# Softmax sums applied to attention's output instead of its weights, with a new order, in attention fused with a gated MLP

## The chip, the cores and the metric

One core of one Trainium2 chip runs the whole program. The metric is device time in microseconds of one execution; lower is better. In texts and rows, PE is TensorE's matmuls, PEld its weight loads, DVE is VectorE, ACT is ScalarE, POOL is GpSimd and SP is the queue that issues all DMAs.

## What is computed

Causal attention over 4 batches, 12 heads, 448 positions and 64 columns a head, then a gated MLP over the 768 joined columns. The inputs q, k and v are float32; w_in and w_out reach the kernel as 64-bit floats.

```
scores = where(mask, -1e9, q k^T / 8);  attn = exp(scores - max)
attn   = attn / (sum(attn) + 1e-9);     x = attn v      (heads joined: 448 x 768)
h = gelu_tanh(x w_in);  u, v = halves of h (512 columns each)
v = (v - mean) / sqrt(var + 1e-6) * g_ln
out = x + (u * (w_sg v + b_sg)) w_out
```

## The kernel before

**Pairs.** Attention runs for two heads at a time (`pair`, 24 pairs, 6 a batch; z is 0 or 1 for the head). The queries of a head lie in four row chunks (`CH`, line 24): 64 rows with 64 keys, then 128 rows each with 192, 320 and 448 keys, so that the part above the diagonal is mostly left out. A pair loads q and k (L438) and v (L533), and TensorE makes the scores into four PSUM banks (L446). VectorE adds the mask in place and takes the maximum (L459), ScalarE takes exp into an SBUF tile P and the sum of each row (L466). Per head, VectorE copies one sum to other partitions (L475), adds 1e-9 (L479), takes the reciprocal of four numbers a partition (L481), and normalises P: two pieces on VectorE, two on GpSimd (L484). Then TensorE transposes P in nine pieces per head (L501, tiles tx and ty): seven of 128 rows, two of 64 rows. ScalarE and VectorE evict them (L508, L510; the bits of `EV` choose), and TensorE multiplies with v into a bank o (L538). ScalarE copies o to xt (L544); xt is written to DRAM (L549), rounded by ScalarE (L551), and GpSimd subtracts the rounded from the exact values (L552, L554), as x is kept as a sum of two parts for the MLP. There are three P tiles.

**Weights.** Each piece of w_in (12) and w_out (8) is loaded as 64-bit words and turned into two float32 parts (`split_w64`): ScalarE scales the high word (L382), VectorE shifts the low word (L384), joins the two (L386) and puts the sign back (L389), ScalarE rounds (L392) and GpSimd subtracts (L393).

**MLP.** For each batch (`mlp`), four token chunks of the v half (66 matmuls), four groups of the u half (72), four groups with w_sg (44) and six groups with w_out (72), all at L571, in pieces of three matmuls, each group in one PSUM bank. The gelu, the mean and variance and the gating run on the other engines (L579 to L584, L621 to L638, L672 to L679); L702 adds x and the result goes out (L706, L710).

**Order.** Nothing runs in the order in which it is written. Each operation is added to a list (`Order.add`) with its engine, an estimated length, what it reads and writes, and a due time. `plan` places them with these estimates: on each engine, of those that are ready, the one that is due first. It also models PSUM banks (`BANKS`, eight in all), the DMA queue and TensorE's pace. The due times come from `STEP` (the distance of pairs by batch), `MLP` and `LEN` (start and length of each batch's MLP) and `DUE` (offsets by kind). The order that results is fixed when the program is built; every engine and the DMA queue then works through its own list in order.

```
STEP = [6.5, 15.0, 15.0, 15.0]
MLP = [-4.9, 2.6, 52.0, 4.0]
BANKS = dict(s=4, tx=1, ty=2, o=1, m=6)
```

Of the kernel before, what the change touches and what calls it, by code (L numbers as in the profile page):

```python
# [9 lines left out]
F32 = mybir.dt.float32  # L10
# [14 lines left out]
    3: (128, 448, 0, 0, 640, 0, 320),  # L25
    0: (64, 64, 0, 448, 1024, 1, 0),
    2: (128, 320, 1, 192, 256, 2, 192),
    1: (128, 192, 1, 0, 0, 3, 64),
}
PW = 1152  # L30

STEP = [6.5, 15.0, 15.0, 15.0]
MLP = [-4.9, 2.6, 52.0, 4.0]
LEN = [80.0, 88.0, 88.0, 53.0]

EV = 9
# [3 lines left out]
NP, XP = 3, 7  # L40
# [3 lines left out]
BANKS = dict(s=4, tx=1, ty=2, o=1, m=6)  # L44

DUE = dict(load=-9, S=-2, mx=-1, ex=2, inv=-2, norm=3, T=4, ev=-2, V=-2, PV=5,
           xo=0, xs=7.5, post=-2, wv=-8.4, wu=40, wo=80, mu=-8.7, ms=11, mo=48)
# [18 lines left out]
class Order:  # L66
# [17 lines left out]
    def add(self, eng, dur, fn, r=(), w=(), at=0.0, done=0.0, rows=1.0, size=0.0, early=0.0, shape=None):  # L84
# [8 lines left out]
        for k in w:  # L93
# [5 lines left out]
            if wr is not None:  # L99
# [5 lines left out]
                             shape=shape,  # L105
# [4 lines left out]
    def plan(self):  # L110
# [72 lines left out]

        def matmul(t, o):
# [10 lines left out]
        while len(order) < len(ops):  # L195
# [23 lines left out]
            if e == "pe":  # L219
                end = matmul(s + (SHIFT if o["shape"] != shape else 0.0), o)  # L220
                shape = o["shape"]
            else:
                end = s + o["d"]
# [36 lines left out]
def attention_gated_mlp(ctx: ExitStack, tc: tile.TileContext, qk, vP, w_in, g_ln, w_sgT, b_sg, w_out, out):  # L260
# [25 lines left out]
    def bank(tag):  # L286
        return Buf(ps, [128, 512], F32, tag, "b")
# [3 lines left out]
    ident = const.tile([128, 128], F32, name="ident")  # L291
    mask = const.tile([128, S], BF16, name="mask")
    gcol = const.tile([128, FC], F32, name="gcol")
# [7 lines left out]
    sm = [const.tile([128, 4], F32, name=f"sm{i}") for i in range(NP)]  # L301
    rs = [const.tile([128, 4], F32, name=f"rs{i}") for i in range(NP)]
# [14 lines left out]
    def dve(n, fn, r, w, at, rate=1.0417, done=0.0):  # L317
        od.add("dve", 0.068 + n * rate / 1000, fn, r, w, at, done)

    def pool_tt(n, fn, r, w, at):  # L320
        od.add("pool", 0.15 + n * 0.0021, fn, r, w, at)

    def pool_ts(n, fn, r, w, at):
        od.add("pool", 0.245 + n * 0.00083, fn, r, w, at)
# [15 lines left out]
    od.add("pool", 1.0, consts, w=["ident", "mask"], at=-9)  # L340

    def consts2():
        for i in range(NP):
            for c in (192, 576, 1088):
                nc.vector.memset(P[i][:, c:c + 64], 0.0)
            nc.vector.memset(sm[i], 1.0)
# [27 lines left out]
    def split_w64(src, dst, key, n, at, pool_, tag, words):  # L374
# [7 lines left out]
        act(n, lambda: nc.scalar.activation(out=f(hi()), in_=f(hi()), func=AF.Copy, scale=2.0 ** -112),  # L382
            [t], [kh], at, True)
        dve(n, lambda: nc.vector.tensor_scalar(out=lo(), in0=lo(), scalar1=29, scalar2=None,  # L384
                                               op0=ALU.logical_shift_right), [t], [kl], at, 0.53)
        dve(n, lambda: nc.vector.scalar_tensor_tensor(out=lo(), in0=hi(), scalar=3, in1=lo(),  # L386
                                                      op0=ALU.logical_shift_left, op1=ALU.bitwise_or),
            [t, kh], [kl], at)
        dve(n, lambda: nc.vector.scalar_tensor_tensor(out=lo(), in0=hi(), scalar=-(2 ** 31), in1=lo(),  # L389
                                                      op0=ALU.bitwise_and, op1=ALU.bitwise_or),  # L390
            [t, kh], [kl], at)
        act(n, lambda: nc.scalar.activation(out=dst(0), in_=f(lo()), func=AF.Copy), [t, kl], [(key, 0)], at, True)  # L392
# [12 lines left out]
    def weights_b():  # L405
# [10 lines left out]
        dve(600, halve, ["gb"], ["gb"], 40)  # L416
# [14 lines left out]
    def pair(p):  # L431
# [9 lines left out]
        def score(cs):  # L441
            for c in cs:
                m, n, bk, col, _, _, q0 = CH[c]
# [9 lines left out]
        for c in (3, 0, 2, 1):  # L453
            m, n, bk, col, off, k, _ = CH[c]
            for z in range(2):
                def mxs(c=c, m=m, n=n, bk=bk, col=col, z=z):
                    o = s[z][bk].t[0:m, col:col + n]
                    mk = mask[0:m, S - n:S] if m == 128 else mask[0:m, S - 128:S - 64]
# [3 lines left out]
        for c in (3, 0, 2, 1):  # L462
            m, n, bk, col, off, k, _ = CH[c]
            for z in range(2):
                i = ib[z]
                act(n, lambda c=c, m=m, n=n, bk=bk, col=col, off=off, k=k, i=i, z=z: nc.scalar.activation(  # L466
# [293 lines left out]
```

## Time and profile before

| | us |
|---|---|
| median of 3 runs (416.07 to 418.93) | 416.31 |
| the profiled execution | 416.54 |
| its span, from first to last instruction | 414.8 |
| busy: TensorE matmul | 388.4 |
| busy: VectorE | 292.1 |
| busy: ScalarE | 224.4 |
| busy: GpSimd | 185.0 |

The mean granted clock of TensorE is 0.967 of full speed over the span. Busy time is time in which an engine executes instructions; a busy TensorE may be one at half clock. Between the profiled execution's time and its span lie 1.7 us at its ends.

### The profile page before, as it was taken

The numbers are of one execution on the slowest core, as the hardware profiler recorded it, in microseconds if no ns is written. First come the engines' busy times: TensorE is split into PE (matmuls) and PEld (weight loads), VectorE is DVE, ScalarE is ACT, GpSimd is POOL, SyncE is SP. The second block draws the span as 40 slices with busy tenths as digits, with TensorE's granted clock in tenths as the row PEclk, the third lists the DMA queues.
The fourth block names the chain that finished last, engine by engine and source line by source line (L and its number), as shares of the span: only waits on it lengthen the run. The fifth ranks groups of instructions, "written<-read, shape, count | busy, mean of one in ns | idle before, by whom it ended". The sixth has DMA issues, their size and how long they took to land.

```text
span 414.8 us, 6860 instructions
## 1 busy us (share of the span) xinstructions
PE 388.4 (94%) x2226; PEld 296.8 (72%) x2226; DVE 292.1 (70%) x926; ACT 224.4 (54%) x625; POOL 185.0 (45%) x236
## 2 busy tenths in 40 slices
PE   7488889897999999999999999999999999999996
PEld 3345555585766767888877866786778789888995
DVE  3999999999998878626768778746858622263622
ACT  2986687764857577513566667635636731133310
POOL 1565656657625955314132675322331655031440
PEclk9598987989899999999999999999999999999999
DMA  7954655710212233530232324455100111400034
GB/s 264 360 161 169 199 173 203 248 56 2 74 56 93 92 94 109 174 128 1 67 112 95 93 55 153 158 155 172 38 27 0 30 63 44 135 2 2 0 129 139
DMA packets 21239, 44.86 MB, mean 108 GB/s; under 512 B 2514, under 2 KB 12498, under 8 KB 21202
## 3 DMA queue, kind: packets, MB, share of 16 engines
q1 hardware_dynamic: 21202, 44.41, 32.8%
q8 instruction: 18, 0.29, 0.3%
q14 instruction: 19, 0.16, 0.1%
HBM read 33.39 MB, written 11.01 MB: 107 GB/s over the span
## 4 chain that ended last, share of the span: by engine, by line
PE 57%; DVE 19%; ACT 11%; POOL 5%; DMA 4%; issue 3%; DVEq 0%; POOLq 0%; ACTq 0%; SPq 0%
PE m L571 38%; ACT P L466 7%; PE s L446 6%; PE o L538 6%; DVE s L459 4%; PE tx L501 3%; DVE P L484 3%; PE ty L501 3%; DMA tmp<-in_w_sgT_dram 2%; ACT ph L510 2%; POOL P L484 1%; DVE vn L386 1%; DMA res<-xd 1%; DVE gT L389 1%; POOL x L552 1%
## 5 line engine op out<-in xcount | busy, mean ns | idle before, releaser
L466 ACT ACTIVATE P<-s,ngm 128x448 f32<-128x448 f32 (+2 forms) x192 | 88.6, 469 | 33.1 <-DVE ngm L459 20.6
L484 POOL TENSOR_SCALAR P<-P,rs 128x384 f32<-128x384 f32 x96 | 57.7, 615 | 99.7 <-DVE rs L481 67.1
L459 DVE CUSTOM_DVE_ANT_0 s<-s,mask 128x448 f32<-128x448 f32 (+2 forms) x192 | 75.6, 444 | 2.0 <-PE s L446 2.0
L571 PE MATMUL m<-win,x 128*128 128x512 f32 (+1 forms) x264 | 69.4, 415 | 2.3 <-POOL x L552 2.1
L571 PE MATMUL m<-x,win 128*128 128x448 f32 x288 | 63.1, 373 | 3.0 <-DVE ph L508 2.3
L571 PE MATMUL m<-gT,wout 128*128 128x448 f32 x288 | 62.6, 369 | 0.0
L571 PEld LDWEIGHTS m<-win,x 128*128 128x128 f32 (+1 forms) x264 | 50.0, 194 | 16.0 <-POOL x L552 2.9
L571 PEld LDWEIGHTS m<-x,win 128*128 128x128 f32 x288 | 54.7, 192 | 8.9 <-DVE ph L508 2.5
L571 PEld LDWEIGHTS m<-gT,wout 128*128 128x128 f32 x288 | 52.8, 188 | 4.7 <-issue 0.4
L538 PE MATMUL o<-ph,vraw 128*64 128x448 f32 (+3 forms) x384 | 53.7, 395 | 0.1
L446 PE MATMUL s<-qk 64*128 64x448 f32 (+3 forms) x384 | 51.9, 406 | 0.0
L538 PEld LDWEIGHTS o<-ph,vraw 128*64 128x64 f32 (+1 forms) x384 | 26.7, 135 | 28.6 <-issue 16.7
L446 PEld LDWEIGHTS s<-qk 64*128 64x128 f32 x384 | 32.2, 188 | 20.6 <-issue 13.0
L501 PE MATMUL ty<-ident,P 128*128 128x128 f32 (+1 forms) x240 | 36.1, 276 | 6.4 <-ACT P L466 3.3
L501 PE MATMUL tx<-ident,P 128*128 128x128 f32 x192 | 32.0, 290 | 9.0 <-DVE P L484 7.8
L571 PE MATMUL m<-wsg,vn 128*128 128x448 f32 x176 | 38.9, 370 | 0.3 <-DVE u L584 0.3
L466 ACT ACTIVATION_READ_ACCUMULATOR P<-s,ngm 128x1 f32 (+1 forms) x192 | 38.3, 199 | 0.0
L484 DVE TENSOR_SCALAR P<-P,rs 128x192 f32<-128x192 f32 x96 | 37.9, 439 | 0.4
L625 POOL TENSOR_TENSOR mv<-mv,mhalf 128x1 f32<-128x1 f32 (+1 forms) x16 | 9.3, 583 | 61.6 <-DVE mv L623 61.5
L702 DVE TENSOR_TENSOR res<-m,res 128x448 f32<-128x448 f32 (+1 forms) x25 | 14.9, 603 | 30.2 <-PE m L571 21.9
L501 PEld LDWEIGHTS ty<-ident,P 128*128 128x128 f32 (+1 forms) x240 | 25.4, 146 | 13.9 <-issue 4.3
L579 ACT ACTIVATE tmp<-m 128x448 f32<-128x448 f32 (+1 forms) x28 | 15.6, 562 | 35.1 <-PE m L571 34.4
(67 smaller groups left out, 521.1 us busy)
## 6 DMA issues: line engine op xcount, KB each, us to landing
qk<-in_qk_dram SPq DMA_DIRECT2D x24, 448.0 KB, 3.9
vn<-in_w_in_dram SPq DMA_DIRECT2D x12, 512.0 KB, 4.8
vraw<-in_vP_dram SPq DMA_DIRECT2D x24, 256.0 KB, 3.0
xd<-xt SPq DMA_DIRECT2D x24, 224.0 KB, 2.9
res<-xd SPq DMA_DIRECT2D x12, 448.0 KB, 3.6
out_dram<-res SPq DMA_DIRECT2D x9, 448.0 KB, 2.6
gT<-in_w_out_dram SPq DMA_DIRECT2D x8, 384.0 KB, 6.7
out_dram<-res SPq DMA_DIRECT2D x5, 224.0 KB, 2.5
```

The lines of the kernel that those rows point to most:

```text
L386: dve(n, lambda: nc.vector.scalar_tensor_tensor(out=lo(), in0=hi(), scalar=3, in1=lo(), op0=ALU.logical_shift_left, op1=ALU.bitwise_or), [ ...
L446: nc.tensor.matmul(out=s[z][bk].t[:, col:col + n], lhsT=qk_.t[r, 0, q0:q0 + 128], rhs=qk_.t[r, 1, 0:n], start=True, stop=True)
L459: nc.vector.tensor_tensor_reduce(out=o, in0=o, in1=mk, scale=-0.125, scalar=3e38, op0=ALU.add, op1=ALU.min, accum_out=ngm[ib[z]][c][0:m])
L466: act(n, lambda c=c, m=m, n=n, bk=bk, col=col, off=off, k=k, i=i, z=z: nc.scalar.activation(out=P[i][0:m, off:off + n], in_=s[z][bk].t[0:m ...
L484: eng.tensor_scalar(out=P[i][:, off:off + n], in0=P[i][:, off:off + n], scalar1=rs[i][:, CH[c][5]:CH[c][5] + 1], scalar2=1.0, op0=ALU.mult ...
L501: nc.tensor.transpose(out, P[i][lo:hi, col:col + 128], ident[lo:hi, lo:hi])
L510: act(512, lambda: nc.scalar.activation(out=pT[z][k].t, in_=tz.t, func=AF.Copy), [tz], [pT[z][k]], Te)
L538: nc.tensor.matmul(out=o.t[r, q0:S], lhsT=vr.t[0:n, c, r], rhs=pT[z][k].t[0:n, lo:hi], start=(c == 0), stop=(c == 3))
L571: nc.tensor.matmul(out=ps.t[0:l().shape[1], 0:n], lhsT=l(), rhs=rr(), start=(k == 0), stop=(k == len(mms) - 1))
L579: act(n, lambda: nc.scalar.activation(out=z(), in_=h(), func=AF.Square), [ps], [t], at)
L625: od.add("pool", 0.46, lambda mv=mv, m=m: nc.gpsimd.tensor_tensor(out=mv.t[0:m, 1:2], in0=mv.t[0:m, 1:2], in1=mhalf[0:m], op=ALU.pow), ["s ...
L702: dve(hi - lo, lambda rr=rr, ps=ps, z=z, lo=lo, hi=hi: nc.vector.tensor_tensor(out=rr.t[:, z, lo:hi], in0=ps.t[:, lo:hi], in1=rr.t[:, z, l ...
```

## The change

The softmax is no longer normalised in P. The sums of a pair's two heads go into one tile (4 chunks, with a column of 1e-9 added in and one column more for a chunk that is summed in two pieces). One reduction and one reciprocal make 16 copies of each head's four reciprocals (128 columns), TensorE transposes them, VectorE copies them out of PSUM, and a DMA writes them to DRAM as 128 rows of 512 bytes. A second DMA reads them back, so that each partition of a head has the factors of all its queries. The product with v, which has queries along its columns, is then multiplied by these factors on its way out of PSUM, in three VectorE instructions instead of one ScalarE copy.

Queries 192 to 255 and 256 to 319 change places on the host, a second mask fits this, and the exp of one chunk is cut into two (five per head instead of four). The layout of P changes with it, so that each head is transposed in eight pieces of 128 rows; three of them use an identity with swapped halves, which puts the columns back. P has four tiles.

In the split of the weights the first step becomes a Prelu with a slope of 2^32 for negative numbers, the sign step goes, and the rounding moves from ScalarE to GpSimd; so does the rounding of x in batch 0. All constants of the order are new, and the planner now lets some GpSimd and VectorE operations exclude each other.

```diff
-STEP = [6.5, 15.0, 15.0, 15.0]
-MLP = [-4.9, 2.6, 52.0, 4.0]
-LEN = [80.0, 88.0, 88.0, 53.0]
-EV = 9
+STEP = [9.31, 12.58, 14.71, 12.64]
+MLP = [9.18, -11.24, 47.82, -79.51]
+LEN = [84.83, 90.85, 44.34, 186.77]
+EV = 10
-NP, XP = 3, 7
+NP, XP = 4, 6
-BANKS = dict(s=4, tx=1, ty=2, o=1, m=6)
+BANKS = dict(s=6, tx=1, ty=1, o=2, m=6)
-DUE = dict(load=-9, S=-2, mx=-1, ex=2, inv=-2, norm=3, T=4, ev=-2, V=-2, PV=5,
-           xo=0, xs=7.5, post=-2, wv=-8.4, wu=40, wo=80, mu=-8.7, ms=11, mo=48)
+DUE = dict(r=17.8, load=-14.54, S=-2.65, mx=-4.52, ex=-0.71, inv=-7.66, Tr=-16.38, T=3.72, ev=-49.43, V=-5.87,
+           PV=12.17, xo=-51.24, xs=18.63, post=4.29, wv=13.56, wu=84.24, wo=73.84, mu=-3.33, ms=14.19, mo=45.14)
...
-        act(n, lambda: nc.scalar.activation(out=f(hi()), in_=f(hi()), func=AF.Copy, scale=2.0 ** -112),
+        act(n, lambda: nc.scalar.activation(out=f(hi()), in_=f(hi()), func=AF.Prelu, scale=2.0 ** -112, alpha=2.0 ** 32),
...
-        dve(n, lambda: nc.vector.scalar_tensor_tensor(out=lo(), in0=hi(), scalar=-(2 ** 31), in1=lo(),
-                                                      op0=ALU.bitwise_and, op1=ALU.bitwise_or),
-            [t, kh], [kl], at)
-        act(n, lambda: nc.scalar.activation(out=dst(0), in_=f(lo()), func=AF.Copy), [t, kl], [(key, 0)], at, True)
+        od.add("pool", 0.13 + n * 0.0012, lambda: nc.gpsimd.tensor_copy(dst(0), f(lo())), [t, kl], [(key, 0)], at, port=True)
...
+        def inv():
+            nc.vector.tensor_reduce(out=tot, in_=sm[ip], op=ALU.add, axis=mybir.AxisListType.X)
+            nc.vector.reciprocal(out=rs.rearrange("p (z n c) -> p z n c", z=2, c=4),
+                                 in_=tot.unsqueeze(2).broadcast_to([128, 2, 16, 4]))
+        od.add("dve", 0.3, inv, sk + ["sm"], ["rs"], T + DUE["inv"])
+        rb, sb = buf(two, "rb", [128, 512]), s[1][1]
+        pe(0.12, lambda: nc.tensor.transpose(sb.t[:, 0:128], rs, ident), ["rs", "ident"], [sb], T + DUE["Tr"])
+        dve(128, lambda: nc.vector.tensor_copy(rT[ip], sb.t[:, 0:128]), [sb], [("rT", ip)], T + DUE["inv"])
+        dma(lambda: nc.sync.dma_start(out=rd[ip], in_=rT[ip]), [("rT", ip)], [("rd", ip)], T + DUE["r"], 65e3)
+        dma(lambda: nc.sync.dma_start(out=rb.t, in_=bass.AP(
+            tensor=rd[ip].tensor, offset=rd[ip].offset, ap=[[512, 32], [0, 4], [1, 512]])), [("rd", ip)], [rb],
+            T + DUE["r"], 262e3)
...
+        for z in range(2):
+            Pk = [("P", ib[z], c) for c in range(5)] + ["ident", "P"]
+            tx, ty = bank("tx"), bank("ty")
+            u = lambda t: t.t.rearrange("p (n q) -> p n q", q=64)
+            pe(0.435, lambda z=z, tx=tx: trans(ib[z], [
+                (u(tx)[:, 0::7, :], 896, ident), (tx.t[:, 64:192], 384, ident), (tx.t[:, 192:320], 0, swap),
+                (tx.t[:, 320:448], 512, ident)]), Pk, [tx], Tt)
+            evict(z, 0, tx)
+            pe(0.435, lambda z=z, ty=ty: trans(ib[z], [
+                (u(ty)[:, 0:6:5, :], 256, swap), (ty.t[:, 64:192], 128, swap), (ty.t[:, 192:320], 640, ident),
+                (ty.t[:, 384:512], 768, ident)]), Pk, [ty], Tt)
+            evict(z, 1, ty)
...
-        act(S, lambda: nc.scalar.activation(out=x.t, in_=o.t[:, 0:S], func=AF.Copy), [o], [x], Tx)
+        def scale():
+
+            def part(a, n, k):
+                two_ = lambda t, c: t[:, c:c + 256 * (k - 1) + n].rearrange("p (u n) -> p u n", n=n)[:, ::256 // n]
+                nc.vector.tensor_tensor(out=two_(x.t, a[0]), in0=two_(o.t, a[0]), in1=two_(rb.t, a[1]), op=ALU.mult)
+            part((64, 128), 128, 2)
+            part((0, 0), 64, 2)
+            part((192, 320), 64, 1)
+        dve(S + 140, scale, [o, rb], [x], Tx)
...
+        if b == 0:
+            od.add("pool", 0.13 + S * 0.0012, lambda: nc.gpsimd.tensor_copy(y.t[:, 0:S], x.t), [x], [y], Ty, port=True)
```

## Rows read from the trace of the kernel before

**Rows 1.** Busy time of each engine, TensorE's clock and DMA in two stretches.
```profile
core 0: us, PE busy (x) PEld busy (x) DVE busy (x) ACT busy (x) POOL busy (x), PEclk, DMA share, GB/s
0.00:125.00 125.00, 103.14 (x575) 69.49 (x577) 114.68 (x353) 85.42 (x236) 70.49 (x85) 0.89 0.49 163
125.00:412.00 287.00, 285.31 (x1653) 227.26 (x1653) 177.39 (x573) 139.02 (x391) 114.55 (x151) 1.00 0.26 84
```
**Rows 2.** Waits of PE, 0 to 125 us: total us, times, longest.
```profile
PE tx L501 <- DVE P L484: 7.8, 2, 7.1
PE ty L501 <- ACT P L466: 3.3, 2, 1.9
PE m L571 <- DVE ph L508: 2.3, 1, 2.3
```
**Rows 3.** Waits of PE, 125 to 412 us: all there are.
```profile
PE tx L501 <- ACT P L466: 0.3, 1, 0.3
```
**Rows 4.** Chain of waits in order of time: start, us, what.
```profile
131.72 2.03 PE o L538 x16
...
137.16 2.04 PE s L446 x16
...
142.04 1.20 PE ty L501 x10
...
336.15 64.60 PE m L571 x310
```
**Rows 5.** Groups of DVE by line, 0 to 125 us: busy, mean ns | idle before.
```profile
L484 DVE TENSOR_SCALAR P<-P,rs 128x192 f32<-128x192 f32 (+1 forms) x32 | 13.5, 476 | 0.0
...
L389 DVE SCALAR_TENSOR_TENSOR vn<-vn 128x512 int32<-128x512 int32 x12 | 9.9, 824 | 0.1
L459 DVE DVE_READ_ACCUMULATOR2_ANT ngm<- 128x1 f32 (+1 forms) x72 | 9.5, 132 | 0.0
...
L389 DVE SCALAR_TENSOR_TENSOR gT<-gT 128x384 int32<-128x384 int32 x8 | 5.4, 689 | 0.0
...
L479 DVE TENSOR_SCALAR rs<-sm 128x4 f32<-128x4 f32 x16 | 3.5, 221 | 0.5 <-ACT P L466 0.4
...
L481 DVE RECIPROCAL rs<-rs 128x4 f32<-128x4 f32 x16 | 2.6, 166 | 0.0
L475 DVE COPY sm<-sm 64x1 f32<-64x1 f32 x18 | 2.5, 150 | 0.8 <-ACT P L466 0.3
```
**Rows 6.** Groups by line and shape, whole span: the last addition, at two widths.
```profile
L702 DVE TENSOR_TENSOR res<-m,res 128x448 f32<-128x448 f32 x23 | 14.3, 622 | 30.2 <-PE m L571 21.9 <-DMA res<-xd 8.2
...
L702 DVE TENSOR_TENSOR res<-m,res 128x224 f32<-128x224 f32 x2 | 0.7, 384 | 0.0
```
**Rows 7.** Groups of ACT by line, 0 to 125 us.
```profile
L392 ACT ACTIVATE win<-vn 128x512 fp32r<-128x512 f32 x12 | 8.2, 688 | 2.8 <-DVE vn L389 2.8
...
L392 ACT ACTIVATE wout<-gT 128x384 fp32r<-128x384 f32 x8 | 4.4, 555 | 4.6 <-DVE gT L389 4.6
...
L544 ACT ACTIVATE xt<-o 128x448 f32<-128x448 f32 x7 | 3.7, 531 | 1.9 <-PE o L538 1.9
...
L382 ACT ACT_TABLE_LOAD x1 | 1.3, 1283 | 0.7 <-PEq L749 0.7
```
**Rows 8.** Groups by line and shape, whole span: the smallest exp.
```profile
L466 ACT ACTIVATE P<-s,ngm 64x64 f32<-64x64 f32 x48 | 14.7, 307 | 0.9
...
L466 ACT ACTIVATION_READ_ACCUMULATOR P<-s,ngm 64x1 f32 x48 | 9.3, 194 | 0.0
```
**Rows 9.** Groups of POOL by line, 0 to 125 us: the two largest.
```profile
L484 POOL TENSOR_SCALAR P<-P,rs 128x384 f32<-128x384 f32 (+1 forms) x32 | 20.8, 667 | 22.6 <-DVE rs L481 13.1 <-DVE rs L479 6.0 <-ACT wout L392 3.6
L393 POOL TENSOR_TENSOR win<-vn,win 128x512 fp32r<-128x512 f32 x12 | 16.0, 1333 | 11.6 <-ACT win L392 11.6
```
**Rows 10.** DMA issues: tensor, queue, times, size, median us from issue to landing.
```profile
xd<-xt SPq DMA_DIRECT2D x24, 224.0 KB, 2.9
```
**Rows 11.** Waits of SP's queue: total us, times, longest.
```profile
SPq L533 <- PE o L538: 99.1, 21, 12.1
```

## What the change should do to the time

> **What bounds the kernel now.** I read the page's slices first, then cut the span where the picture changes. Two stages appear [rows 1]. Up to 125 us VectorE is busy 114.7 us, or 92%, while TensorE's matmuls cover 103.1 us at a mean granted clock of 0.89. From 125 to 412 us TensorE is busy 285.3 of 287 us at clock 1.00 and VectorE only 62%. So the first stage goes at VectorE's pace, with TensorE idle for 22 us and at half clock after its idle times, and the second at TensorE's. Next, the waits of TensorE in the first stage: they are spread, with the largest, 7.8 us, on the normalisation of P [rows 2], and in the second stage there is one of 0.3 us [rows 3]. The chain of waits gives full-clock prices: a pair's PV 2.03 us, its scores 2.04, ten transposes 1.20 (0.12 each), and 310 matmuls of the MLP 64.60 (0.208 each) [rows 4].
>
> From these I estimate TensorE's full-clock work: 24 pairs x (2.03 + 2.04 + 18 x 0.12 = 6.23) = 150 us and 4 batches x 254 MLP matmuls (66 + 72 + 44 + 72 by the code) x 0.208 = 212, in all 361. The second stage holds 285 of it, so the first holds about 76, with the warm-up and shape switches about 84. It takes 125: 41 us are lost there, and only there.
>
> **The change part by part.**
>
> *VectorE, removed.* In the first stage, 32 normalisations of P (8 pairs) took 13.5 us, the sign step of the weight split 9.9 and 5.4, the two steps to the reciprocal 3.5 and 2.6, and the copy of a sum 2.5 [rows 5]: 37.4 us, all on the engine that sets the pace.
>
> *VectorE, added, per pair.* A PSUM operand with an SBUF one took 622 ns at 448 columns and 384 at 224 [rows 6], so 1.06 ns a column over a fixed 0.146. The scaling in three parts of 256, 128 and 64 columns is 0.42 + 0.28 + 0.21 = 0.91 us; the copy of 128 columns 0.28; the sum of 24 numbers some 0.20, as a step on 4 numbers did. The reciprocal now makes 128 results, and the trace has it on 4 only: 166 ns [rows 5]. From below: all fixed but 1.06 ns an element, 0.30 us. From above: whatever it has over the cheapest VectorE instruction, the 132 ns accumulator read, is per element: 34/4 = 8.5 ns, so 0.13 + 1.09 = 1.2 us. The pair costs 1.7 to 2.6 us. The trace cannot choose, so I take the middle, 2.15.
> The Trainium skill, "VectorE: DVE Perf Modes", section "First, the fixed hardware budget", speaks for the upper end: it says that the reciprocal is an iterative division with a repeat count of 8. From its 0.96 GHz that is an estimated 1.07 us for 128 results; the 8.5 ns an element that I took as the bound agrees with it, but rows on 4 elements cannot settle it. By the rule the sum below would be 396.5 instead of 392.5.
>
> *First stage.* 114.7 - 37.4 + 8 x 2.15 (17.2) = 94.5 us of VectorE. At the same 92% that is 103 us instead of 125: -22. The ends: 90.9/0.92 = 99 (-26) and 98.1/0.92 = 107 (-18).
>
> *ScalarE.* It loses the rounding copies of the weights (8.2 + 4.4 us) and the copies of o (3.7) [rows 7], and batch 0's rounding of x. It gains a fifth exp per head: a 64-column exp is 307 ns and its accumulator read 194 [rows 8], overlapping a little, against 128 columns less in the one that was cut; at most 0.5 us a head, 8 us over 8 pairs. From 85.4 it goes to about 77 of 103 us: beside VectorE.
>
> *GpSimd.* The norms go (20.8 us). The 20 rounding copies and 6 of x come. No row has a copy there: from 0.67 us, a norm's mean, to 1.33, a two-input subtraction [rows 9], so 17 to 35 us; I take 0.75, being a one-input operation, 19.5. GpSimd stays at about 70 us (86 at the upper end) of 103. If that cover is gone, the weights come late and rival 3 follows. The two new masks and the swapped identity are made in the first microseconds, while TensorE warms up on zeros and the loads run: nothing. The order of q's rows is made on the host: nothing.
>
> *TensorE.* Two transposes a pair go, and one (of the reciprocals) comes: 0.12 us saved. From -0.1 (the lone transpose between scores pays switches that the halves paid before) to 0.3. In the second stage, 16 pairs: 1.9 us, and this comes through, as nothing else sets the pace there. In the first it is hidden behind VectorE. Transposes no longer wait for the reciprocal and its norms: the 7.1 us wait at the start shortens. That is part of the 22, not beside it.
>
> *DMA and the new wait.* Each pair adds a 64 KB write and a broadcast read that waits for it. The write of x (224 KB) lands after 2.9 us [rows 10]; two in series are about 5.8 and with transpose and copy 6.5 us after the sums. The weighted sum takes 16 x 0.12 + one eviction + 2.03, about 4.7 us, from the same moment, so o may wait some 2 us for its factors. Behind the scaling on VectorE's queue stand the next pair's masks and evictions. Two o banks and the planner's later place for the scaling (its due time was fitted to the DMA) cover it: I cost it at nothing, at most 2 us x 8 pairs in stage one, where VectorE would stand. In stage two VectorE has 38% free. SP already stands in waits for most of the run, up to 12.1 us before a load of V [rows 11]; a factor behind such a load would come that late. One of the four score banks is kept about 1 us longer per pair: covered by six being allowed now.
>
> *The order.* All due times, spacings and banks change. From -8 (TensorE is never starved but at the start) to +22 (none of VectorE's relief arrives); I take nothing, as the same planner makes it.
>
> **Sum.** 416.54 (the profiled run; its span is 414.8, 1.7 us lie around it) - 22 - 1.9 = 392.6. This run is 0.2 above the median of three; I say 392.5. The tail after the last matmul, 3 to 4 us, stays.
>
> **The rivals.**
>
> 1. *TensorE takes over at once.* If VectorE's load is also spread (pairs of batch 0 are now placed 9.3 instead of 6.5 apart), stage one is TensorE's 84 us plus the start, where it has only scores until the first P is there (the 7.1 us wait of rows 2 and some 2 us at half clock, about 9): 93 instead of 125. 416.5 - 32 - 2 = 383; with some idle time left 384. For it: 41 us of loss in the stage. Against: VectorE would still have to be 98% busy if its work is 91. Chance 0.17.
> 2. *Factors late on VectorE.* 2 us x 8 pairs / 0.92 = 17 us of the 22 are given back: about 408. For it: two DMAs in series are longer than the path to o. Against: 62% in stage two and the due times. Chance 0.09.
> 3. *Another chain sets the first stage* (GpSimd's rounding of the weights, or a score bank): its length stays within a few us, 412 to 418. For it: the waits of rows 2 are on P from two engines and on an eviction, not on one thing. Chance 0.06.
> 4. *Slower: SP's queue.* The loads of V waited 4.7 us on average (99.1/21) and the factors' read stands in the same in-order queue. If it stands behind such a load each time, VectorE's queue, blocked by the scaling, loses 8 x 4.7/0.92 = 41 us in stage one: 392.5 + 41 = 433. It decides from 24 us given back, 2.8 us per pair. Against: due times place the reads, and the planner models this queue. Chance 0.04.
> 5. *Slower: table loads.* The split's first step becomes Prelu. The trace shows one table load of 1.28 us for Exp, Tanh, Square and Copy together [rows 7]. If Prelu stood in another table, 20 splits between exps would cost up to 40 loads, 51 us: ScalarE 77 + 51 = 128, at 92% 139 us for stage one: 416.5 + 14 - 2 = 429. Chance 0.04. The Trainium skill, "ScalarE: Activation LUTs", section "Table sets: the hidden batching unit", says that each change of set costs a load and that cheap functions stand in every set; it does not list Prelu. No row of this trace shows it either way.
>
> **How the numbers follow.** The main case has 0.60: 392.5, its own range 387 to 399 (reciprocal's ends, transposes' ends, a little of the order). With rivals 1 and 2 that is 0.86 faster by over 1%, which is about what a measurement of this kernel can tell from no change; rival 3 is 0.06 within 1%; rivals 4 and 5 are 0.08 slower. The range reaches from 383 (rival 1) to 408 (rival 2).
>
> **What would show it.** Right: VectorE's busy total falls from 292 to about 262 (norms, reciprocals and sum copies were 22.1 us for 8 pairs, so -66 for 24; -15.3 for the sign step; +52); the stretch in which TensorE idles or runs below clock 1.00 ends near 103 us; TensorE's busy total falls by the half-clock time; one table load. Wrong: TensorE waiting on the scaling or on a DMA of the factors; VectorE idle before the scaling by over 10 us in all; the last matmul less than 10 us earlier; reciprocals above 1.2 us.

## The result, and the profile after

The changed kernel takes 403.55 us (median of 4, 401.22 to 403.96) beside 417.16 for the kernel before on the same chip: ratio 0.966, 95% interval 0.960 to 0.971. The forecast was 392.5 with a range of 383 to 408. The direction is right and the time lies in the range, but of the forecast 5.7% only 3.4% came. In this part a difference in microseconds between two versions is that of their ratios times 417.2; with the intervals it is good to some 2 or 3 us.

Busy time in stretches of the changed kernel, to set beside [rows 1]:

```profile
0.00:125.00 125.00, 112.17 (x677) 73.78 (x677) 110.26 (x360) 88.62 (x297) 69.77 (x88) 0.95 0.63 207
125.00:399.00 274.00, 268.96 (x1529) 214.71 (x1527) 161.55 (x453) 124.93 (x374) 76.83 (x84) 1.00 0.31 97
...
25.00:40.00 15.00, 9.31 (x50) 4.83 (x49) 8.67 (x37) 9.17 (x35) 7.38 (x9) 0.77 0.70 221
40.00:125.00 85.00, 82.49 (x528) 57.60 (x528) 82.81 (x249) 62.67 (x209) 53.62 (x62) 1.00 0.58 186
125.00:380.00 255.00, 250.55 (x1441) 198.20 (x1440) 156.34 (x444) 123.19 (x371) 70.83 (x79) 1.00 0.30 94
```

The first 125 us now hold 677 matmuls instead of 575, and what follows is 12.8 us shorter (277.0 us of the span instead of 289.8): that is the whole gain. From 40 to 125 us TensorE is 97% busy at full clock, while VectorE is 97% busy too. What is lost lies in three places: the start to 40 us, 2.5 us from there to 125, and, new, 5 us after 125, where the kernel before lost 1.7 of 287.

The waits of TensorE over the whole span (total us, times, longest), beside [rows 2, 3]:

```profile
PE s L506 <- DVE rs L502: 4.7, 11, 0.8
PE s L470 <- DVE xt L561: 4.5, 1, 4.5
...
PE s L506 <- ACT P L491: 1.7, 4, 0.5
```

L506 is the lone transpose of the reciprocals, L502 the reciprocal, L561 the scaling. Of the 4.7 us, 1.7 lie in the first 125 us and 3.0 after them. The normalisation has gone from the list, and the new path has come in its place.

The groups by line and shape, beside [rows 5, 6, 7, 9]:

```profile
L502 DVE RECIPROCAL rs<-tot 128x128 f32<-128x128 f32 x24 | 22.9, 953 | 0.8
...
L561 DVE TENSOR_TENSOR xt<-o,rb 128x256 f32<-128x256 f32 x24 | 10.0, 416 | 9.7 <-DMA rb<-rd 5.7 <-PE o L549 2.8 <-issue 1.1
...
L416 POOL CAST win<-vn 128x512 fp32r<-128x512 f32 x12 | 9.2, 768 | 23.3 <-DVE vn L413 22.0 <-DVE mv L647 1.3
...
L411 DVE TENSOR_SCALAR vn<-vn 128x512 int32<-128x512 int32 x12 | 8.4, 717 | 1.2 <-DMA vn<-in_w_in_dram 1.2
...
L507 DVE COPY rT<-s 128x128 f32<-128x128 f32 x24 | 6.8, 284 | 2.7 <-PE s L506 2.7
L561 DVE TENSOR_TENSOR xt<-o,rb 128x128 f32<-128x128 f32 x24 | 6.6, 277 | 0.0
...
L561 DVE TENSOR_TENSOR xt<-o,rb 128x64 f32<-128x64 f32 x24 | 5.1, 210 | 0.0
...
L501 DVE TENSOR_REDUCE tot<-sm 128x8 f32<-128x24 f32 x24 | 4.1, 173 | 7.5 <-ACT P L491 7.2
...
L409 ACT ACT_TABLE_LOAD x1 | 1.3, 1283 | 0.7 <-PEq L775 0.7
```

Per pair VectorE has 0.17 + 0.95 + 0.28 + 0.90 = 2.31 us new. One table load: Prelu costs none.

The start, in the timeline of SP's queue (start, us, what) and in the chain (start, us):

```profile
15.42 0.33 SPq L406 DMA_DIRECT2D vn<-in_w_in_dram  x1
16.98 0.33 SPq L508 DMA_DIRECT2D rd<-rT  x1
22.48 0.70 SPq L394 DMA_DIRECT2D tmp<-in_w_sgT_dram  x1
23.29 0.56 SPq L509 DMA_DIRECT2D rb<-rd  x1
```
```profile
23.29 9.24 DMA rb<-rd
```

The first factors are written at 17 us. Their read stands behind a load that waits for a buffer until 22.5, and lands only 9.2 us after it is issued. VectorE stands for it 5.7 us, TensorE 4.5 us, and the clock of 25 to 40 us is 0.77.

### The profile page after: what moved, and what is told of

Read it like the earlier page. It is cut to its first block, busy times and chain, and to the rows that moved or that the text cites. A ratio compares the mean times of both kernels' runs of the same rounds, so it can differ in the third digit from the quotient of the medians.

```text
span 402.0 us, 6733 instructions
## 1 busy us (share of the span) xinstructions
PE 381.1 (95%) x2202; PEld 288.5 (72%) x2202; DVE 271.9 (68%) x812; ACT 213.5 (53%) x671; POOL 146.6 (36%) x171
## 4 chain that ended last, share of the span: by engine, by line
PE 64%; DVE 15%; ACT 10%; DMA 4%; issue 4%; POOL 1%; SPq 0%; DVEq 0%; ACTq 0%; POOLq 0%
PE m L595 43%; ACT P L491 7%; PE o L549 7%; PE s L470 6%; DVE s L483 4%; PE tx L518 3%; PE ty L518 3%; DMA rb<-rd 2%; DVE rs L502 2%; DVE vn L411 2%; DVE ph L523 2%; DMA vn<-in_w_in_dram 2%; ACT ph L525 1%; PE m L387 1%; PE s L506 1%
## 5 line engine op out<-in xcount | busy, mean ns | idle before, releaser
L491 ACT ACTIVATE P<-s,ngm 64x64 f32<-64x64 f32 (+3 forms) x240 | 100.0, 425 | 45.0 <-DVE ngm L483 40.7
L595 PE MATMUL m<-win,x 128*128 128x512 f32 (+1 forms) x264 | 65.9, 401 | 0.0
L470 PE MATMUL s<-qk 64*128 64x448 f32 (+3 forms) x384 | 54.5, 414 | 4.5 <-DVE xt L561 4.5
L595 PEld LDWEIGHTS m<-win,x 128*128 128x128 f32 (+1 forms) x264 | 47.4, 184 | 12.2 <-issue 0.2
L491 ACT ACTIVATION_READ_ACCUMULATOR P<-s,ngm 128x1 f32 (+1 forms) x240 | 47.5, 198 | 0.0
L549 PEld LDWEIGHTS o<-ph,vraw 128*64 128x64 f32 (+1 forms) x384 | 23.4, 137 | 28.6 <-issue 20.5
L576 POOL TENSOR_TENSOR x<-xt,x 128x448 fp32r<-128x448 f32 x24 | 28.4, 1183 | 37.6 <-ACT x L575 37.0
L523 DVE COPY ph<-ty 128x512 f32<-128x512 f32 x48 | 32.6, 679 | 10.8 <-PE ty L518 10.7
L525 ACT ACTIVATE ph<-tx 128x512 f32<-128x512 f32 x48 | 28.5, 595 | 14.4 <-PE tx L518 14.0
L595 PEld LDWEIGHTS m<-wsg,vn 128*128 128x128 f32 x176 | 31.8, 189 | 2.3
L518 PE MATMUL tx<-ident,P 128*128 128x128 f32 x144 | 30.4, 282 | 2.5 <-ACT P L491 1.3
```

The lines of the kernel that those rows point to most:

```text
L470: nc.tensor.matmul(out=s[z][bk].t[:, col:col + n], lhsT=qk_.t[r, 0, q0:q0 + 128], rhs=qk_.t[r, 1, 0:n], start=True, stop=True)
L491: act(n, lambda c=c, m=m, r0=r0, k0=k0, n=n, bk=bk, col=col, off=off, kc=kc, i=i, z=z: nc.scalar.activation(out=P[i][r0:m, off:off + n], i ...
L518: nc.tensor.transpose(out, P[i][:, col:col + 128], idn)
L523: dve(512, lambda: nc.vector.tensor_copy(pT[z][k].t, tz.t), [tz], [pT[z][k]], Te)
L525: act(512, lambda: nc.scalar.activation(out=pT[z][k].t, in_=tz.t, func=AF.Copy), [tz], [pT[z][k]], Te)
L549: nc.tensor.matmul(out=o.t[r, q0:S], lhsT=vr.t[0:n, c, r], rhs=pT[z][k].t[0:n, lo:hi], start=(c == 0), stop=(c == 3))
```

## The experiments

| run | us | ratio to before, interval | against the change |
|---|---|---|---|
| the change | 403.55 | 0.966 [0.960, 0.971] | |
| e1 reciprocal of 8, spread | 401.26 | 0.960 [0.956, 0.963] | -2.6 |
| e2 first factors earlier | 403.90 | 0.966 [0.962, 0.971] | 0 |
| e3 no factor path | 386.08 | 0.923 [0.920, 0.927] | -17.7 |
| e4 sign step back | 413.32 | 0.988 [0.985, 0.992] | +9.3 |
| e5 weights later | 397.78 | 0.952 [0.949, 0.956] | -5.7 |
| e6 no factor DMAs | 401.36 | 0.962 [0.958, 0.966] | -1.6 |
| e7 no lone transpose | 396.65 | 0.949 [0.944, 0.954] | -7.1 |
| e8 eight rows | 442.17 | 1.058 [1.052, 1.064] | +38 |
| e9 old constants | 411.36 | 0.984 [0.981, 0.987] | +7.5 |
| e10 no sum, no reciprocal | 391.60 | 0.937 [0.935, 0.940] | -11.8 |
| e11 weights later, reciprocal of 8 spread by ScalarE | 396.49 | 0.948 [0.946, 0.951] | -7.3 |
| e12 weights later, planner told | 398.86 | 0.954 [0.951, 0.957] | -4.8 |

**e1.**
```diff
+    rec = const.tile([128, 2, 4], F32, name="rec")
...
-            nc.vector.reciprocal(out=rs.rearrange("p (z n c) -> p z n c", z=2, c=4),
-                                 in_=tot.unsqueeze(2).broadcast_to([128, 2, 16, 4]))
+            nc.vector.reciprocal(out=rec, in_=tot)
+            nc.vector.tensor_copy(rs.rearrange("p (z n c) -> p z n c", z=2, c=4),
+                                  rec.unsqueeze(2).broadcast_to([128, 2, 16, 4]))
```


> Edit: the reciprocal is taken of the 8 sums of a pair and a copy spreads it to 128, instead of a reciprocal of 128; the order of all operations is the same. The reciprocal took 953 ns, the copy should take about 0.2 us, so VectorE has some 0.55 us less per pair. Theory A (the step that was mis-sized is VectorE's price of the reciprocal: the transpose of it stands in TensorE's queue, and TensorE waits 4.7 us in 11 places for it, and VectorE still sets the pace of the first 125 us): these waits fall under 1.5 us, 8 pairs x 0.55 = 4.4 us come off the first stage, and the time falls to 396 to 399. Rival B (TensorE paces already, and what it waits for at those places is exps or the pairs themselves): the waits only change their names and the time stays at 402 to 404.

Between the two: 2.6 us, which the intervals do not tell from nothing, with the waits before the lone transpose at 3.5 us. The copy did not take 0.2 us. In the groups of the whole span, in those of the first 125 us, and in the timeline:

```profile
L504 DVE COPY rs<-rec 128x128 f32<-128x128 f32 x24 | 11.5, 480 | 0.8
...
L503 DVE RECIPROCAL rec<-tot 128x8 f32<-128x8 f32 x24 | 4.9, 203 | 0.8
```
```profile
L504 DVE COPY rs<-rec 128x128 f32<-128x128 f32 x11 | 7.6, 690 | 0.4
```
```profile
244.18 1.14 POOL L578 TENSOR_TENSOR x<-xt,x 128x448 fp32r<-128x448 f32 x1 [7.40 <-ACT x L577]
244.19 1.21 DVE L504 COPY rs<-rec 128x128 f32<-128x128 f32 x1
```

A copy that starts together with a GpSimd subtraction ends just after it, at 1.21 us. Nine of the 24 copies took 0.43 to 1.29 us. Each of them started while a GpSimd instruction was running (eight subtractions and one cast) and ended within 0.1 us of its end; the other 15 took 0.23 us. The Trainium skill, "SBUF — State Buffer", section "Who interferes with whom", has the rule: a VectorE copy can enter a mode that uses the port pair shared with GpSimd, and whichever of the two is issued first then has the pair for its whole instruction. The trace agrees, by these nine copies.

Over the whole run VectorE won 0.27 us a pair (0.95 against 0.20 + 0.48). But eight of the nine slow copies lie in the first 125 us, where it won only 0.06 (0.95 against 0.20 + 0.69). So e1 took next to nothing off VectorE in the stage that mattered, and says little about the worth of VectorE's time there.

**e2.** The read of the first pair's factors is issued one place earlier in SP's queue.
```diff
-        for n in self.plan():
+        order = self.plan()
+        i = order.index(self.first)
+        j = max(k for k in range(i) if self.ops[order[k]]["e"] == "sp")
+        order.insert(j, order.pop(i))
+        for n in order:
...
+        if p == 0:
+            od.first = len(od.ops) - 1
```


> Edit: in the DMA queue the read of the first pair's factors changes places with the load of a piece of w_sg that stood before it; nothing else moves. In the changed kernel this read was issued at 23.3 us, 5.1 us of it behind that load's wait for a GpSimd buffer, landed 9.2 us later, and VectorE and then TensorE stood for it (5.7 and 4.5 us), after which the clock was at half for about 8 us. Theory A (rival 4 of the prediction, once, at the start): the factors land 4 to 6 us earlier, the wait shrinks below 1 us, the clock stays up, and the time falls by 5 to 8 us, to 395 to 399. Rival B (the start's loss is absorbed, since VectorE sets the pace up to 125 us whatever happens at 30): at most 2 us. Rival C: the DMA engines are full there, so the read lands as late as before and nothing changes.

No gain. The read was issued only at 23.6 us, as it waited 6.1 us for the written factors to land, and the start's wait became one for v:

```profile
PE o L555 <- DMA vraw<-in_vP_dram: 5.4, 1, 5.4
```

So the transfer that is late first only stands for the crowded start as a whole; C comes nearest.

**e3.** Sum, reciprocal, lone transpose, copy and both DMAs are no longer issued.
```diff
-        od.add("dve", 0.3, inv, sk + ["sm"], ["rs"], T + DUE["inv"])
...
+        def inv():
+            pass
+        od.add("dve", 0.3, inv, sk + ["sm"], ["rs"], T + DUE["inv"])
```


> Leaves out the division by the sums: reciprocal, its transpose, the copy and both DMAs are not issued, o is multiplied with a constant tile; all other operations keep their order. Theory A (the factors' path is what the prediction under-priced): the 7.5 us of waits before the lone transposes, the start's wait of 4.5 us with its half clock, and 1.4 us of VectorE per pair go: 385 to 390. Rival B (the missing 11 us lie in the new order of the pairs and the MLP, not in the path): 397 to 403, and TensorE waits elsewhere.

Theory A: 386.1. Its stretches have no gap at all from 40 us on:

```profile
40.00:125.00 85.00, 85.00 (x552) 61.59 (x548) 78.91 (x244) 66.17 (x224) 54.37 (x62) 1.00 0.50 162
125.00:380.00 255.00, 255.00 (x1465) 208.11 (x1464) 137.98 (x385) 117.78 (x353) 72.81 (x80) 1.00 0.25 82
```

So the new order leaves TensorE nothing to wait for; the path of the factors costs 17.7 us.

**e4.** The sign step on VectorE and the plain copy instead of Prelu are back.
```diff
-        act(n, lambda: nc.scalar.activation(out=f(hi()), in_=f(hi()), func=AF.Prelu, scale=2.0 ** -112, alpha=2.0 ** 32),
+        act(n, lambda: nc.scalar.activation(out=f(hi()), in_=f(hi()), func=AF.Copy, scale=2.0 ** -112),
...
+        dve(n, lambda: nc.vector.scalar_tensor_tensor(out=lo(), in0=hi(), scalar=-(2 ** 31), in1=lo(),
+                                                      op0=ALU.bitwise_and, op1=ALU.bitwise_or),
+            [t, kh], [kl], at)
```

> Edit: the split of the weights gets the sign step on VectorE back (20 instructions, 15.3 us in the kernel before) and the plain copy instead of Prelu; the planner is told and orders anew. Theory A (VectorE sets the pace of the first 125 us of the changed kernel too, so what the prediction took off it at 92% counts): +10 to +16 us, 413 to 419. Rival B (TensorE or ScalarE paces by now and VectorE has room): +0 to +4 us, 403 to 407.

+9.3 us for 16.1 us of VectorE's instructions: just under A's range, and far from B. VectorE's time in the first stage still counts, at 0.58 us for each, not one for one. The records of VectorE's instructions overlap, so that a group's durations add up to more than the busy time that goes with the group: of the 16.1 us, 12.8 are time in which no other VectorE instruction ran. Against these the rate is 0.73. The planner ordered anew here, so either rate holds for these two orders only.

**e5.**
```diff
-        dma(lambda: nc.sync.dma_start(out=t.t[:, :n], in_=src), [], [t], at - 6, n * 512)
+        dma(lambda: nc.sync.dma_start(out=t.t[:, :n], in_=src), [], [t], at - 6, n * 512, 45)
...
-                                      in_=src.bitcast(I32)), [], [t], at - 6, n * 1024)
+                                      in_=src.bitcast(I32)), [], [t], at - 6, n * 1024, 45 if tag == "gT" else 0.0)
```


> Edit: the loads of w_sg and w_out may not be issued before 45 us of the planner's time (they were issued from 3.5 us on, among the first pairs' loads); the planner orders anew. The run with the read of the first factors moved alone lost no time at the start and gained none: the wait for the factors became a wait of 5.4 us for v, since the DMA queue was at full load there. Theory A (the start is bound by DMA traffic that is not needed yet): the waits at 25 to 35 us go, the clock stays up, and the time falls by 4 to 8 us to 395 to 400. Rival B (a loss at the start is made up by 125 us, as VectorE sets the pace): 401 to 404.

Theory A by the time: -5.7 us. The planner ordered everything anew, so this is the gain of the later loads together with their order. Nor was the DMA queue quite at full load, as the expectation has it: in the change the DMA engines were busy 0.79 of the time to 25 us and 0.70 from 25 to 40 us. The stretch that had 9.31 us of matmuls at 0.77:

```profile
25.00:40.00 15.00, 13.78 (x99) 8.37 (x99) 14.63 (x55) 12.18 (x48) 10.68 (x12) 1.00 0.79 261
```

**e6.**
```diff
-        dma(lambda: nc.sync.dma_start(out=rd[ip], in_=rT[ip]), [("rT", ip)], [("rd", ip)], T + DUE["r"], 65e3)
+        dma(lambda: None, [("rT", ip)], [("rd", ip)], T + DUE["r"], 65e3)
...
-                in1=two_(rb.t, a[1])
+                in1=two_(ones, a[1])
```


> Leaves out the two DMAs of the factors (o is multiplied with a constant tile); reciprocal, transpose and copy stay, and so does the order. Without the whole path the time was 386.1. Theory A (most of the 17.5 us that the path costs is the lone transpose in TensorE's queue and the long reciprocal): the DMAs are worth 3 to 6 us, at the start only: 397 to 401. Rival B (it is the DMA traffic and the waits of other loads behind it): 386 to 392.

Nearer to theory A than to B, but under A's 3 to 6 us: the DMAs alone are worth 1.6 us, which the intervals do not tell from nothing.

**e7.**
```diff
-        pe(0.12, lambda: nc.tensor.transpose(sb.t[:, 0:128], rs, ident), ["rs", "ident"], [sb], T + DUE["Tr"])
-        dve(128, lambda: nc.vector.tensor_copy(rT[ip], sb.t[:, 0:128]), [sb], [("rT", ip)], T + DUE["inv"])
+        pe(0.12, lambda: None, ["rs", "ident"], [sb], T + DUE["Tr"])
+        dve(128, lambda: nc.vector.tensor_copy(rT[ip], rs), [sb], [("rT", ip)], T + DUE["inv"])
```


> Leaves out the transpose of the reciprocals (the copy reads them untransposed, so the factors are wrong); reciprocal, copy and both DMAs stay, and so does the order. Theory A (TensorE loses 0.3 to 0.5 us at each of the 24 lone transposes, in waits before it and in its own slot, where the prediction had 0.12): 7 to 12 us less, 392 to 397. Rival B (VectorE's reciprocal costs as VectorE time, whoever waits for it): 400 to 403.

Theory A: 7.1 us, 0.30 us for each lone transpose, slot and waits together. The edit also made the copy dearer, as it now reads SBUF (0.41 us on average instead of 0.28), so the transpose may cost a little more than this. After 125 us TensorE has no gap:

```profile
125.00:380.00 255.00, 255.00 (x1470) 204.35 (x1469) 159.19 (x450) 124.48 (x377) 76.29 (x85) 1.00 0.30 97
```

**e8.**
```diff
-            nc.vector.reciprocal(out=rs.rearrange("p (z n c) -> p z n c", z=2, c=4),
-                                 in_=tot.unsqueeze(2).broadcast_to([128, 2, 16, 4]))
+            nc.vector.reciprocal(out=rs, in_=tot.rearrange("p z c -> p (z c)"))
...
-            tensor=rd[ip].tensor, offset=rd[ip].offset, ap=[[512, 32], [0, 4], [1, 512]])), [("rd", ip)], [rb],
+            tensor=rd[ip].tensor, offset=rd[ip].offset, ap=[[512, 2], [0, 64], [1, 512]])), [("rd", ip)], [rb],
```


> Edit: the 16 copies are undone. The reciprocal is of 8 numbers, the transpose gives 8 rows of 128, 4 KB are written, and the read takes each row for 64 partitions; the order stays. VectorE has 0.75 us less per pair and no copy between the reciprocal and the transpose. Theory A (the long reciprocal stands between the sums and TensorE): the 4.7 us of waits go and VectorE gains 8 x 0.75 = 6 us in the first stage: 394 to 398. Rival B (16 copies are needed, because a read of the same 2 KB by 64 partitions is slow): the reads take over 6 us instead of 3.2, VectorE waits for them, and the time is 404 or more. Rival C (no gain, as with the reciprocal of 8 and a copy: 2.3 us): 400 to 402.

Rival B by the time, and by far, but not for the reason that it gives. The read is of the same size, but of two rows of 2 KB instead of 32. SP's issues and the scalings that waited for them (start, us, what, idle before):

```profile
24.08 0.50 SPq L508 DMA_DIRECT2D rb<-rd  x1
...
39.35 0.51 SPq L508 DMA_DIRECT2D rb<-rd  x1
```
```profile
38.00 0.75 DVE L560 TENSOR_TENSOR xt<-o,rb 128x256 f32<-128x256 f32 x3 [11.89 <-DMA rb<-rd]
48.68 0.75 DVE L560 TENSOR_TENSOR xt<-o,rb 128x256 f32<-128x256 f32 x3 [3.54 <-DMA rb<-rd]
```

13.9 and 9.3 us from issue to the scaling. Over the 24 reads the median from issue to landing is 8.4 us, against 3.2 with the copies.

The packets were not slower. In both runs a read is 128 packets of 2 KB, and packets of 2 KB took 84 ns at the median. But a read that stood alone, issued at 241.07 us, had two packets under way at a time and never more than three, from 1.3 to 7.0 us after its issue. One of the change, issued at 212.18 us, had up to 19 under way, from 1.3 to 2.5 us. The landing of each read is reported by 16 updates in the change, and in e8 by two, after one that came before any packet. So two DMA engines seem to have worked where 16 did, and the edit went along with that: it made the outermost count of the read's access pattern 2 instead of 32. That reading the same bytes for 64 partitions is slow in itself is not shown. A read of the eight rows with an outermost count of 16 or more was not tried, so the 38 us are what this layout costs, and not what the 16 copies are worth.

**e9.** STEP, MLP, LEN and the due times of the kernel before, in the changed kernel; the two new kinds at `r=2, Tr=0`.
```diff
-STEP = [9.31, 12.58, 14.71, 12.64]
-MLP = [9.18, -11.24, 47.82, -79.51]
-LEN = [84.83, 90.85, 44.34, 186.77]
+STEP = [6.5, 15.0, 15.0, 15.0]
+MLP = [-4.9, 2.6, 52.0, 4.0]
+LEN = [80.0, 88.0, 88.0, 53.0]
...
-DUE = dict(r=17.8, load=-14.54, S=-2.65, mx=-4.52, ex=-0.71, inv=-7.66, Tr=-16.38, T=3.72, ev=-49.43, V=-5.87,
-           PV=12.17, xo=-51.24, xs=18.63, post=4.29, wv=13.56, wu=84.24, wo=73.84, mu=-3.33, ms=14.19, mo=45.14)
+DUE = dict(r=2, Tr=0, load=-9, S=-2, mx=-1, ex=2, inv=-2, norm=3, T=4, ev=-2, V=-2, PV=5,
+           xo=0, xs=7.5, post=-2, wv=-8.4, wu=40, wo=80, mu=-8.7, ms=11, mo=48)
```

> Edit: the changed kernel with STEP, MLP, LEN and DUE of the kernel before (the two new kinds get due times 0 and 2); banks and all operations as changed. The prediction costed the new order at nothing, between -8 and +22. If the new constants are worth nothing: 402 to 406. If the gain comes from them: 412 or more. If they hide part of it: 400 or less.

411.4, between the first two readings and close to the second: the operations alone, with the old constants, bring 1.6%, and the new constants the rest. The old ones were not fitted to the new operations, and the two due times were a guess, so 7.5 us is what this pair of sets differs by, not what an order in general is worth.

**e10.** Sum and reciprocal are not issued.
```diff
+        nc.vector.memset(rs, 0.0044)
...
-            nc.vector.tensor_reduce(out=tot, in_=sm[ip], op=ALU.add, axis=mybir.AxisListType.X)
-            nc.vector.reciprocal(out=rs.rearrange("p (z n c) -> p z n c", z=2, c=4),
-                                 in_=tot.unsqueeze(2).broadcast_to([128, 2, 16, 4]))
+            pass
```

> Leaves out the sum and the reciprocal on VectorE (1.12 us per pair; the factors are a constant that is transposed, copied and sent as before); the order stays. Of the 17.5 us that the whole path costs, the DMAs took 2.2 alone and the transpose 6.9 alone. Theory A (VectorE sets the pace of the first 125 us, and the transposes there wait for the reciprocal): 8 pairs x 1.12 = 9 us off VectorE's first stage and the waits for it: 393 to 397. Rival B (VectorE's time has cover; only the transpose counts): 400 to 403.

11.8 us, more than the 9 that A had. Not 8 pairs lie in the first 125 us of the changed kernel but 11 (11 reciprocals of 10.5 us there), so VectorE loses 12.3 us of instructions in them. Part of the gain lies elsewhere: after 125 us the waits for the reciprocal go, and with them TensorE's gaps, which were 4.5 us to 380 in the change.

```profile
125.00:380.00 255.00, 255.00 (x1475) 206.68 (x1472) 143.60 (x411) 121.22 (x364) 75.25 (x83) 1.00 0.30 96
```

That leaves about 7 us for the first 125 us, or 0.6 us for each of VectorE's, as in e4.

The three parts, taken out alone, make 1.6 + 7.1 + 11.8 = 20.5 us, and together 17.7. The waits before the lone transposes are in two of them, and the copy is in none; with 2 or 3 us on each, the difference is not clear of noise.

**e11.** With e5's edit as well:
```diff
-            nc.vector.reciprocal(out=rs.rearrange("p (z n c) -> p z n c", z=2, c=4),
-                                 in_=tot.unsqueeze(2).broadcast_to([128, 2, 16, 4]))
-        od.add("dve", 0.3, inv, sk + ["sm"], ["rs"], T + DUE["inv"])
+            nc.vector.reciprocal(out=rec, in_=tot)
+        od.add("dve", 0.37, inv, sk + ["sm"], ["rec"], T + DUE["inv"])
+        act(128, lambda: nc.scalar.activation(out=rs.rearrange("p (z n c) -> p z n c", z=2, c=4),
+                                              in_=rec.unsqueeze(2).broadcast_to([128, 2, 16, 4]), func=AF.Copy),
+            ["rec"], ["rs"], T + DUE["inv"], True)
```


> Edit: the later loads of w_sg and w_out (397.8 alone), and the reciprocal of 8 numbers on VectorE spread to 128 by a ScalarE copy instead of a reciprocal of 128; the planner is told these lengths and orders anew. Theory A (VectorE's time in the first stage and the transpose's wait for it are what is left of the path's price): 0.75 us less per pair on VectorE, 6 us in the first stage, and shorter waits: 390 to 394. Rival B (ScalarE's queue delays the spread copy, as exps stand in it): waits before the lone transpose on ScalarE, 396 to 400.

396.5, the fastest version that leaves nothing out (0.948), but its interval overlaps that of e5. After 125 us no wait is left; a wait of 4.4 us for exps and a half clock stretch came between 40 and 125 us, in an order that the planner made anew. Neither theory is decided.

**e12.** With e5's edit as well, the planner is told a length of 1.12 us for the sum and reciprocal:
```diff
-        od.add("dve", 0.3, inv, sk + ["sm"], ["rs"], T + DUE["inv"])
+        od.add("dve", 1.12, inv, sk + ["sm"], ["rs"], T + DUE["inv"])
```


> Edit: the later loads of w_sg and w_out, and the planner is told that sum and reciprocal take 1.12 us, not 0.3; the operations are the same. Theory A (TensorE waits before the lone transposes because the planner thinks that the reciprocal is there 0.8 us earlier): the 5.0 us of waits on it fall under 2 and the time to 393 to 396. Rival B (the wait only moves, as VectorE's time is what is short): 397 to 399.

Rival B. The waits for the reciprocal did fall, from 5.0 to 0.9 us, and the time did not:

```profile
PE s L506 <- DVE rs L502: 0.9, 2, 0.5
```
```profile
40.00:125.00 85.00, 77.77 (x470) 53.80 (x469) 75.07 (x215) 57.91 (x183) 50.48 (x56) 0.98 0.61 204
```

From 40 to 125 us only 470 matmuls ran, against 523 in e5: what is no longer waited for late is missing early.

## Why the prediction was right, and only in part of its size

**Two stages, and VectorE sets the pace of the first: right.** Taking work off VectorE there shortened the kernel, and e4 and e10 show it from both sides. But the sum turned VectorE's time into kernel time at 1/0.92 = 1.09; e4 and the first stage of e10 measured about 0.6. A smaller part of this is how the sum was made. It took the busy times of groups, 37.4 us, from VectorE's busy total, but the records overlap: in the first 125 us of the kernel before they add up to 142.0 us, in 114.7 us of busy time. The removed groups have only 30.4 us there in which nothing else ran, and the new ones in the change 1.6 us a pair, not 2.31. The two errors nearly cancel, by luck: 114.7 - 30.4 + 8 x 1.6 = 97 us where the forecast had 94.5. The rest goes with the next limit: from 40 to 125 us TensorE itself is at 97%, as rival 1 had it for the whole stage. No run isolates that.

**VectorE's price per pair: right.** 2.31 us beside 2.15 taken and 1.7 to 2.6 as bounds. The scaling came at 0.90 (0.91), the copy at 0.28 (0.28), the sum at 0.17 (0.20). The reciprocal is 0.95 us, nearer the upper bound: (953 - 203)/(128 - 8) = 6.25 ns an element by the shapes of e1, where the bound had 8.5 and one column of an addition 1.06. From the repeat count of 8 in the Trainium skill, "VectorE: DVE Perf Modes", section "First, the fixed hardware budget", the prediction had estimated 1.07 us for 128 results, 8.3 ns each. That was the right side, and the measured 6.25 decides on the size. The upper bound held, but it was less safe than it looked: the accumulator read of 132 ns is not the cheapest of VectorE's instructions (a memset of one column took 59 ns in the kernel before).

**The step that was mis-sized: the path of the factors.** Without it the forecast's own numbers give rival 1's floor, 384: VectorE's 77.3 us and 8 scalings make 92 us at 92%, and TensorE's stage has 93. e3 measured 386.1. With the path the forecast added 8.5 us to that floor, the chip 17.7. Two steps of the prediction under-priced it:
- "Two transposes a pair go, and one (of the reciprocals) comes: 0.12 us saved", coming through as -1.9 in the second stage. The lone transpose is not 0.12 us but 0.30 (e7): it stands in TensorE's queue behind a chain of sums, sum step and a reciprocal of nearly a microsecond, and everything after it in the queue stands with it, after 125 us too, where the change has 4.5 us of gaps to 380 and e7 none. The prediction named what stands behind the scaling on VectorE, and not what stands behind the transpose on TensorE.
- The reciprocal was charged to 8 pairs of the first stage, as many as lay there in the kernel before. In the changed kernel 11 lie in the first 125 us (e10), and 10 with the old constants (e9). The stage did not end sooner; it holds more.

**"The order ... I take nothing": wrong in one way.** e9 gives the new constants 7.5 us over the old ones, within the stated -8 to +22. It also means that the operations alone, with constants not fitted to them, brought 7 us where the sum had 24.

**The new DMAs at nothing: nearly right** (e6, 1.6 us; the write lands in 1.7 us, the read in 3.2, where 2.9 each were taken). Rival 4, a read that stands in SP's queue behind a load, happened once, at the start. It looked like the cause of 5 us there, but e2 and e6 show the same loss with another name; e5, in which the order is new as well, points to the early weight loads. These were in the kernel before as well, and the prediction left the start inside the 22.

**Rival 2: its time, not its cause.** Its 408 lies nearest to the measured time, but VectorE stood for the factors once, 5.7 us at the start, and not at every pair; without the DMAs only 1.6 us are won. The main case's own range ended at 399, so that the time lies in the stated range only because rival 2's price stretched it: that is luck. By its own sum rival 2 should have said 410 (392.5 + 17), as GpSimd's upper end should have been 85 us and not 86; neither changes what is said here.

**Rivals 3 and 5: no.** GpSimd's casts took 0.77 and 0.64 us (0.75 taken) and nobody waited long for them; Prelu needed no second table.

**The signs named beforehand.** VectorE's total fell to 271.9 us, not 262: what was removed had 64.8 us with no other VectorE instruction running, where the sums had 81, and what is new has 43.5, where they had 52. Of the signs of being wrong, TensorE did wait on the scaling, once, for 4.5 us; VectorE stood before it for 9.7 us in all, just under the 10 named. TensorE's total fell from 388.4 to 381.1. The last matmul came 12.6 us earlier, just over the 10 named. The stretch below full clock ended at 40 us, not near 103, since more work now lies in the first stage, which did not end sooner.

**Open.** Why the exchange rate of VectorE's time is about 0.6, what a set of constants fitted to e11's operations would bring, and what a read of eight rows would cost if all DMA engines shared it: no run shows it.

## What to carry to other kernels

When work leaves the pace-setting engine, price what replaces it where it stands in the queue of every engine that it passes: a 0.1 us instruction that waits on another engine's chain costs the whole queue behind it. Before changing the layout of a broadcast read or of copies that look wasteful, measure the read, and count how many of its packets are under way at once. And when a named wait sits at a crowded start, try moving the traffic, not the transfer that happens to be late.

## What the runs showed of the hardware that was not expected

- A DMA read of 256 KB into SBUF landed 8.4 us after its issue (median) when its access pattern had a count of 2 outermost, with two packets under way at a time, and 3.2 us after it with a count of 32 and up to 19 packets under way. Packets of 2 KB took 84 ns at the median in both (e8).
- The reciprocal on VectorE costs 6.25 ns for each further element between the two shapes measured (953 ns for 128, 203 for 8).
- VectorE's shift of the weights, from SBUF to SBUF, lasts longer when it starts beside a running GpSimd subtraction, until some 0.3 us after that has ended. In the change this happened to four of 12 (1.19 to 1.46 us; the other eight took 0.41 to 0.42), in the kernel before to two (0.88 and 1.12), which is why the mean rose from 521 to 717 ns. Copies of 128 columns that started so in e1 ended within 0.1 us of the subtraction's end (0.57 to 1.29 us, against 0.23 alone).
